# RetNet attention then SwiGLU, one core: five places for raw weights, other places of loads, stores and one product in the order of work

## The chip, the cores and the metric

The kernel runs on one core of a Trainium2 chip. The metric is the device time in microseconds (us) of one execution; times of several executions are given as a median with lowest and highest. A profile is one more execution with the hardware profiler on: it gives a span (first to last instruction) and every instruction's start and duration. The engines are TensorE (PE in the profile; its weight loads PEld), VectorE (DVE), ScalarE (ACT), GpSimd (POOL), and SyncE (SP), which here only issues transfers (its queue is SPq). Each engine works through its own list of instructions in order; a transfer is issued by a queue in order, too, and an instruction that waits holds everything behind it on that engine.

## The reference

Eight batches, eight heads, 576 positions, head size 64. All in 32-bit floats:

```python
scores = (q @ k.T) / 8                        # per batch and head
ret    = scores * gamma[h] ** (i - j)         # for i >= j, else 0
x      = ret @ v                              # -> (4608, 512), heads side by side
xn     = x / sqrt(mean(x*x) + 1e-6) * rms_g   # by row
g, val = xn @ w_gate, xn @ w_val              # 512 -> 1536
out    = (g * sigmoid(g) * val) @ w_out       # 1536 -> 512
```

## The kernel before

**Attention.** A job is one batch and a pair of heads: 32 jobs, numbered 0 to 31. A `slot(j)` (line 403) does `values(j-1)` (347, the product of weighted scores and v), `scores(j)`, `states(j)`, `weigh(j)` and then `carried(j-1)` (366), which adds the part that comes from earlier chunks of 64 positions, multiplies by the decay and writes the x of its unit of 512 tokens. `close(j)` (417) is values and carried of the last job of a batch. Carried must not begin before values has ended; this is told by a tiny copy named `tick` (361, 363): on GpSimd for jobs 0 to 7, on ScalarE afterwards. The loads of jobs 0 to 7 are issued at the start (`load_first`, `load_tails`); a later job is brought in by `fetch(j)` (421: 4 transfers for q, 4 for k in another layout, 2 for k, 2 for v, 1 for v's tail `vt`) and made ready by `prepare(j)` (251: two transposes on VectorE, four scalings of v on ScalarE by line 265). There is one place each for the raw q and k, so a fetch also waits for the prepare before it.

**Units.** Tokens are taken in nine units u of 512. Units 2 to 8 use Strassen-like products: `up(u, n)` (580) with seven products on precombined blocks of the gate and value weights, then `across(u)` (703) with seven pieces of the output weights. Those precombined blocks lie in device memory (`w_up_blocks`, `w_out_blocks`) and are loaded into a ring by `refill` (550), on SyncE, whenever a place is free. Units 0 and 1 are what the change is about.

**The plain stage.** The weights must first be rounded and combined, and units 0 and 1 meanwhile use plain products. The raw weights are cut into 36 half chunks (line 825): sets `up 0` to `up 5` of gate and value blocks and slices `out 0` to `out 2` of the output weights, four half chunks each. `load_half` (840) brings one raw half chunk into one of a few places, `spare`. Then, on VectorE: `exponent` (863), two activations on ScalarE (860), `mantissa` (877, three instructions), `join` (894, line 907). `rounding` (955) hands this out in steps; the order in it is: exponent of the next half chunk, mantissa of this one, join of this one. So three steps are one half chunk, and after join i the load for a later half chunk is issued by SyncE. When the fourth half chunk of a set or slice has been joined, GpSimd forms the sums (line 918; four instructions for a set, eight for a slice, through `finish_set` and `finish_slice`), and some joins later SyncE issues the stores to device memory (`store_blocks`, 937). All slices share one place in `vi`, and so the join of the next slice waits until the stores of the one before have landed.

The order of the work is written out by hand in `start()` (994); no planner is at work. First come slots 0 to 7 with some steps of rounding between (`weights(n)`). Then the twelve blocks of `up_plain(u, k)` (639) for units 0 and 1, four groups each, 48 in all; `now` numbers them. A group is four products of 128x128 by 512 columns; the profile shows a matmul as two records, so a group is eight records. For odd k VectorE multiplies the group's result (656), for even k ScalarE applies Silu (658). After each group come `weights(3)` and two activations; `weights_to(READY[k])` makes sure that the set for the block is joined. In the code:

```python
weights(3 if now > 3 else 1)
act(2)
if i == 1:
    weights_to(READY[k])
```

Some groups are followed by a prepare, a fetch or a slot for the jobs 8 to 11. After block (0, 5), that is after group 39, the rest of rounding and the last stores are put on the queues and then the first refill; the fetch of job 11 stands behind these on SyncE, after group 41, and job 11 is prepared after group 44 and has its slot after group 45. After group 47 comes the close of job 11, and `across(0)`.

**Later units.** For u = 2 to 6, `up(u, n)` with n = 0 to 3 is followed by a slot each, and n = 4 by the close of the last job of that batch (line 1144).

Of the kernel before, what the change touches and what calls it, by code (L numbers as in the profile page):

```python
# [10 lines left out]
F32 = mybir.dt.float32  # L11
# [30 lines left out]
def kernel(  # L42
# [44 lines left out]
    def bank(name):  # L87
        return banks.tile([P, 512], F32, tag="b", name=name)
# [7 lines left out]
    def cell(name, value):  # L96
# [34 lines left out]
    AT_SETS, N_SETS = NF * U, 3  # L131
    AT_SUMS = AT_SETS + N_SETS * 4 * BLOCK
    AT_RAW = AT_SUMS + 4 * BLOCK
    WORDS, SLOT = 2 * 4 * P, 3 * 4 * P
    assert AT_RAW + 2 * SLOT <= RING
    spare = [
        ring[:, AT_RAW : AT_RAW + SLOT], ring[:, AT_RAW + SLOT : AT_RAW + 2 * SLOT],
        t1.rearrange("p f t -> p (f t)"), sums_x.rearrange("p i c t -> p (i c t)"),
    ]

    A11, A12, S1, A22, S2, S3, S4 = range(7)
    A21 = 7
# [274 lines left out]
    def close(j):  # L417
        values(j)
        carried(j)

    def fetch(j):
        if j < len(jobs):
            load_qk(j)
            load_kv(j)
# [107 lines left out]

    UP, OUT = 7 * 2 * 2 * P, 7 * NK * P
    w_up_d = dram.tile([2 * NG, P, UP], F32, name="w_up_blocks")
    w_out_d = dram.tile([7, P, 7, NK, P], F32, name="w_out_blocks")
    ORDER = (A11, S1, S3, S2, A12, S4, A22)
    pieces = [("out", u, n) for u in range(2) for n in range(7)]
    for u in range(2, NU):
# [11 lines left out]
    def refill(most=len(pieces)):  # L550

        nonlocal n_sent
        while n_sent < min(most, len(pieces)):
            a, z = places[n_sent]
            if any(a < y and x < z for x, y in places[n_used:n_sent]):
                return
            kind, u, n = pieces[n_sent]
            src = w_up_d[n] if kind == "up" else w_out_d[ORDER[n]].rearrange("p n c d -> p (n c d)")
            nc.sync.dma_start(out=ring[:, a:z], in_=src)
            n_sent += 1  # L560

    def piece(kind, u, n):
        assert pieces[n_used] == (kind, u, n) and n_used < n_sent
        a, z = places[n_used]
        if kind == "up":
            return ring[:, a:z].rearrange("p (b c f) -> p b c f", b=7, c=2)
        return ring[:, a:z].rearrange("p (n c d) -> p n c d", n=7, c=NK)

    def used():
        nonlocal n_used  # L570
# [253 lines left out]
    slices = vi[:, : 49 * P].rearrange("p (o n d) -> p o n d", o=7, n=7)  # L824
    halves = []
    for kind, at in (
        ("up", 0), ("up", 1), ("up", 2), ("out", 0), ("up", 3), ("out", 1), ("up", 4), ("up", 5),
        ("out", 2),
    ):
        halves += [(kind, at, a, c) for a in range(2) for c in range(2)]  # L830

    def words_of(i):
        return spare[i % 4][:, :WORDS].bitcast(U32)

    exps = {}

# [25 lines left out]

    def exponent(i):

        exps[i] = bank(f"exp_{i}") if in_psum else spare[i % 4][:, WORDS:]
        w, e = words_of(i), exp_of(i).bitcast(U32)
        nc.vector.tensor_scalar(
            out=e, in0=w[:, 1::2], scalar1=20, scalar2=0x7FF,
            op0=ALU.logical_shift_right, op1=ALU.bitwise_and,
        )  # L870
        f = exp_of(i)
        acts.extend((i, x) for x in (
            dict(out=f, in_=e, bias=most, scale=-1.0),
            dict(out=e, in_=f, bias=top, scale=-(2.0**23)),
        ))
# [56 lines left out]
    def finish_slice(k):  # L932
        combine_blocks([slices[:, i, :4] for i in range(7)], S1)
        combine_blocks([slices[:, :, i] for i in range(7)], S1)
        stores.append((n_joined + 5, [(w_out_d[o][:, :, k], slices[:, o]) for o in ORDER]))

    def store_blocks(n):

# [16 lines left out]
    def rounding():  # L955

        nonlocal n_joined
        exponent(0)
        yield
        for i in range(len(halves)):  # L960
            if i + 1 < len(halves):
                exponent(i + 1)
            yield
            mantissa(i)
            yield
            while not free_for(*halves[i][:2]):
                assert not due
                yield
            join(i)
            n_joined += 1  # L970
            store_blocks(n_joined)
            load_half(i + 4, nc.sync)
            yield

    steps = rounding()
# [1 line left out]
    def weights(n):  # L977

        for _ in range(n):
            next(steps, None)  # L980
# [6 lines left out]
            next(steps)  # L987
        due = False

    READY = (4, 8, 12, 20, 28, 32)  # L990

    def start():
# [12 lines left out]
        warm_up(6)  # L1007
        for i in (1, 0, 2):
            table(i, nc.scalar)
        load_half(0, nc.scalar)  # L1010
        for j in range(FIRST):
            load_first(j)
            if j == 0:
                load_tails(0, range(2))
                table(3, nc.sync)
            elif j == 1:
                load_tails(0, range(2, H))
                load_half(1, nc.sync)
            elif j == 5:
                load_half(3, nc.sync)  # L1020
            elif j == 3:
                load_half(2, nc.sync)
                nc.sync.dma_start(out=rms_g, in_=moe_rms_g.rearrange("(c p) -> p c", p=P))
            elif j == 4:
                load_tails(1, range(H))
                table(4, nc.sync)
        turn(0, 1)
        scale_v(0)
        squares = []
        weights(1)  # L1030
        for j in range(FIRST):
            slot(j, rest=(j > 0))
            if j + 1 < FIRST:
                turn(j + 1)
            if squares:
                gather(*squares.pop())
            for i in ((1,), (2,), (3,), (4, 5), (6,), (7,), (), ())[j]:
                scale_v(i)
            if j:
                squares.append((*divmod(j - 1, NHP), square(*divmod(j - 1, NHP))))  # L1040
            act(1)
            if j == 5:
                norm_1(0)
            elif j == 6:
                norm_2(0)
            weights((1, 1, 2, 2, 1, 1, 1, 1)[j])
            if j == 4:
                gather(*squares.pop())
            elif j == 5:
                diagonals(0)  # L1050
            act(1)
# [4 lines left out]
        for u, k in (  # L1056
            (0, 0), (1, 0), (0, 1), (1, 1), (0, 2), (1, 2), (0, 3), (1, 3), (0, 4), (0, 5), (1, 4),
            (1, 5),
        ):
            weights_to(READY[k] - 2)  # L1060
            for i, _ in enumerate(up_plain(u, k)):
                if now == 0:
                    close(FIRST - 1)
                    gather(1, NHP - 1, square(1, NHP - 1))
                elif now == 1:
                    norm_1(1)
                elif now == 2:
                    diagonals(1)
                elif now == 3:
                    norm_2(1)  # L1070
                elif now in (10, 16):
                    prepare(FIRST + (now - 10) // 6)
                elif now in (12, 18):
                    fetch(FIRST + 1 + (now - 12) // 6)
                elif now == 34:
                    slot(FIRST, rest=False)
                elif now in (40, 42, 45):
                    slot(FIRST + {40: 1, 42: 2, 45: 3}[now])
                elif now in (41, 44, 46):
                    n = {41: 2, 44: 3, 46: 4}[now]  # L1080
                    prepare(FIRST + n)
                    fetch(FIRST + n + 1)
                elif now == 47:
                    close(FIRST + NHP - 1)
                weights(3 if now > 3 else 1)
                act(2)
                if i == 1:
                    weights_to(READY[k])
                now += 1
            sets_used[k] += 1  # L1090
            if (u, k) == (0, 5):
                weights_to(len(halves))
                store_blocks(len(halves) + 9)
                refill(1)
            elif (u, k) == (1, 4):
                refill(2)
                for f in range(0, NH, 2):
                    differences(0, f)
                inner_sums(0, 0)
                inner_sums(0, 1)  # L1100
# [22 lines left out]
    with tc.manual_schedule():  # L1123
        start()
        for u in range(2, NU):
            j0 = NHP * (u + 1)
            more = u + 1 < B
            for n in range(2 * NG):
                for i, _ in enumerate(up(u, n)):
                    if n == 1 and i == 4:  # L1130
                        store(u - 1)
                    if more and i == 2 and 0 < n <= NHP:
                        if j0 + n < len(jobs):
                            prepare(j0 + n)
                            fetch(j0 + n + 1)
                    if u + 1 < NU and n == 2 * NG - 1:
                        if i < NHP:
                            gather(u + 1, i, square(u + 1, i))
                        elif i == NHP:
                            root_1(u + 1)  # L1140
                if more and n < NHP:
                    slot(j0 + n, rest=(n > 0))
                elif more and n == NHP:
                    close(j0 + NHP - 1)
            for i, _ in enumerate(across(u)):
                if u + 1 == NU:
                    continue
# [33 lines left out]
```

## Time and profile before

| | us |
|---|---|
| median of 8 runs (lowest, highest) | 1160.27 (1158.23, 1163.93) |
| the profiled execution's own time | 1161.05 |
| its span | 1159.3 |
| TensorE busy | 1108.3 (96%) |
| VectorE busy | 822.0 (71%) |
| GpSimd busy | 400.5 (35%) |
| ScalarE busy | 247.8 (21%) |
| mean granted TensorE clock | 0.982 |

How to read it. The slices show the span in 40 equal parts of 29 us; each digit is the busy share in tenths, 9 for 90% or more; PEclk is the clock that TensorE was granted, in tenths of full speed. In a list of instructions in order of time, a row has the start, the duration, engine, line, operation, what it writes and reads, the shape, how many instructions are merged in it, and in brackets how long the engine was idle before the first of them and what ended that. A merged row runs from its first start to its last end. TensorE's instructions overlap, so a row ends 0.28 us after the next product could have begun. VectorE's instructions of 128x512 are shown with 0.69 us but start 0.60 apart. In a row of SPq the duration is that of issuing, not of the transfer.

### The profile page before, as it was taken

How to read it: one execution, taken by the hardware profiler on the slowest of the kernel's cores; microseconds unless marked ns; L12 is line 12 of the kernel's file. 1: busy time of each engine (PE TensorE's matmuls, PEld its weight loads, DVE VectorE, ACT ScalarE, POOL GpSimd, SP SyncE). 2: the span in 40 equal slices, each digit the busy share in tenths (PEclk: the TensorE clock that was granted, in tenths of full speed). 3: DMA queues.
4: the chain of work that ended last, by engine and by line, in shares of the span. 5: the costliest groups of instructions: out<-in, count | busy, mean ns of one | idle time of the engine just before them, and what ended most of it. 6: DMA issues, size and time to landing. Idle time of an engine off the chain costs nothing. (4 is left out here: it accounts for less than half of the span.)

```text
span 1159.3 us, 24137 instructions
## 1 busy us (share of the span) xinstructions
PE 1108.3 (96%) x10086; PEld 919.4 (79%) x10086; DVE 822.0 (71%) x1426; ACT 247.8 (21%) x501; POOL 400.5 (35%) x328
## 2 busy tenths in 40 slices
PE   7899777998999999999999999999999999999997
PEld 6744333457998889888988899889988998898897
DVE  4899857667696769576947795779576954593465
ACT  5534422211002120123012301221212111201110
POOL 0023524543752018301730164006500660174035
PEclk9999888998999999999999999999999999999999
DMA  8648898388887887578668875897576556475461
GB/s 211 158 111 259 223 292 265 117 217 252 313 305 228 233 246 252 159 202 217 265 210 222 247 247 183 196 256 265 191 178 238 194 194 223 143 272 177 159 238 38
DMA packets 255421, 249.22 MB, mean 215 GB/s; under 512 B 193104, under 2 KB 232656, under 8 KB 241104
## 3 DMA queue, kind: packets, MB, share of 16 engines
q1 hardware_dynamic: 253456, 246.59, 68.5%
q8 instruction: 79, 1.29, 0.5%
q10 hardware_dynamic: 1856, 1.09, 0.3%
q14 instruction: 30, 0.25, 0.1%
HBM read 217.55 MB, written 30.08 MB: 214 GB/s over the span
## 5 line engine op out<-in xcount | busy, mean ns | idle before, releaser
L701 POOL TENSOR_TENSOR vi<-h 128x384 f32<-128x384 f32 x64 | 77.6, 1229 | 502.5 <-DVE h L608 456.8
L650 PE MATMUL up<-x,ring 128*128 128x512 f32 x384 | 178.0, 622 | 19.9 <-DVE ring L656 9.2
L650 PEld LDWEIGHTS up<-x,ring 128*128 128x128 f32 x384 | 74.9, 199 | 117.6 <-issue 85.0
L589 PE MATMUL x<-x,ring 128*128 128x256 f32 x672 | 161.5, 383 | 0.8 <-issue 0.8
L589 PE MATMUL z<-x,ring 128*128 128x256 f32 x672 | 158.8, 379 | 0.0
L589 PE MATMUL w<-sums,ring 128*128 128x256 f32 x672 | 158.7, 379 | 0.0
L589 PEld LDWEIGHTS z<-x,ring 128*128 128x128 f32 x672 | 127.7, 190 | 19.9 <-issue 2.9
L589 PEld LDWEIGHTS w<-sums,ring 128*128 128x128 f32 x672 | 127.7, 190 | 17.4
L589 PEld LDWEIGHTS x<-x,ring 128*128 128x128 f32 x672 | 125.1, 190 | 18.4 <-issue 1.0
L589 PE MATMUL y<-sums,ring 128*128 128x256 f32 x336 | 79.4, 379 | 0.0
L802 POOL TENSOR_TENSOR vi<-vi 128x512 f32<-128x512 f32 (+1 forms) x56 | 67.2, 1213 | 22.1 <-DVE vi L748 19.6
L596 DVE TENSOR_TENSOR h<-u,w 128x512 f32<-128x512 f32 x42 | 28.9, 688 | 61.1 <-PE w L589 61.1
L589 PEld LDWEIGHTS y<-sums,ring 128*128 128x128 f32 x336 | 63.8, 190 | 8.7
L615 ACT COPY m<-x 128x512 f32<-128x512 f32 x42 | 24.6, 586 | 189.1 <-PE x L589 189.1
L596 DVE TENSOR_TENSOR u<-m,y 128x512 f32<-128x512 f32 x42 | 28.8, 686 | 50.2 <-PE y L589 50.2
L333 DVE SCALAR_TENSOR_TENSOR sum<-sum,gc,s 128x64 f32<-128x64 f32 x192 | 53.9, 281 | 6.8
L610 ACT ACTIVATE h<-h 128x512 f32<-128x512 f32 x63 | 39.7, 630 | 79.8 <-DVE h L596 79.8
L918 POOL TENSOR_TENSOR vi<-vi 128x512 f32<-128x512 f32 (+1 forms) x24 | 40.3, 1681 | 45.8 <-DVE vi L907 20.5
L744 ACT COPY vi<-xo 128x512 f32<-128x512 f32 x18 | 10.6, 587 | 211.3 <-PE xo L730 178.6
L596 DVE TENSOR_TENSOR u<-u,z 128x512 f32<-128x512 f32 x42 | 28.9, 687 | 26.7 <-PE z L589 25.7
L701 POOL TENSOR_TENSOR vi<-h,vi 128x384 f32<-128x384 f32 x32 | 46.3, 1447 | 2.5
L918 POOL TENSOR_TENSOR ring<-ring 128x512 f32<-128x512 f32 x24 | 30.5, 1278 | 46.8 <-DVE sums L890 31.2
(252 smaller groups left out, 2001.1 us busy)
## 6 DMA issues: line engine op xcount, KB each, us to landing
ring<-w_out_blocks SPq DMA_DIRECT2D x63, 1344.0 KB, 6.7
ring<-w_up_blocks SPq DMA_DIRECT2D x42, 1792.0 KB, 7.9
w_out_blocks<-vi SPq DMA_DIRECT2D x21, 448.0 KB, 6.0
out_dram<-vi SPq DMA_DIRECT2D x64, 128.0 KB, 3.1
qraw<-in_q_dram SPq DMA_DIRECT2D x96, 72.0 KB, 5.2
kraw<-in_k_dram SPq DMA_DIRECT2D x96, 72.0 KB, 3.1
k<-in_k_dram SPq DMA_DIRECT2D x48, 128.0 KB, 3.0
v<-in_v_dram SPq DMA_DIRECT2D x48, 128.0 KB, 3.0
```

The costliest lines, as they stand in the source:

```text
L333: nc.vector.scalar_tensor_tensor(out=t[:, c], in0=t[:, c - 1], scalar=gc[:, hp : hp + 1], in1=part, op0=ALU.mult, op1=ALU.add,)
L589: nc.tensor.matmul(ps[:, i * HU : i * HU + HU], lhsT=w[:, PLACE[blk], c, i * P : i * P + P], rhs=t_of[u][blk][:, c], start=(start and i == ...
L596: nc.vector.tensor_tensor(out=o, in0=a, in1=pairs_of(ps), op=ALU.add)
L610: nc.scalar.activation(out=o, in_=c, func=AF.Silu)
L615: nc.scalar.copy(out=s1, in_=pairs_of(x_))
L650: nc.tensor.matmul(ps, lhsT=w[:, PLACE[blk], c % 2, i * P : i * P + P], rhs=x_of[u][:, c], start=(c == 0), stop=(c == NHP - 1),)
L701: eng.tensor_tensor(out=o, in0=a, in1=b, op=op)
L744: nc.scalar.copy(out=o, in_=ps)
L802: eng.tensor_tensor(out=t[:, :, o], in0=t[:, :, x], in1=t[:, :, y], op=ALU.add)
L918: nc.gpsimd.tensor_tensor(out=t[o], in0=t[x], in1=t[y], op=op)
```

## The change

- The raw weights have five places instead of four, each without room for its exponents; before the exponents go to PSUM, they use two other places in turn. A load is then issued five half chunks ahead.
- The order of half chunks: slice `out 0` comes before set `up 2` instead of behind it, so half chunks 8 to 11 instead of 12 to 15. `READY` is adjusted for `up 2`.
- `w_out_blocks` is laid out with the slice ahead of the partition: a store of a slice writes 128 rows of 3584 B instead of 896 rows of 512 B, and a refill reads three rows per partition instead of one.
- At the start, half chunk 0 is loaded by SyncE behind the loads of job 1 instead of by ScalarE ahead of all; the other first loads move too, and the tails of jobs 4 to 7 come one job sooner.
- The steps of rounding are dealt out otherwise: none by slots 0 and 1, then 1, 2, 2, 2, 1, 2; in the plain stage two and three in turn instead of three.
- `prepare(8)` and `fetch(9)` move from groups 10 and 12 to group 28; `prepare(9)` and `fetch(10)` from 16 and 18 to 36.
- In units 2 to 6, the values of a batch's last job are issued ahead of the last product of `up(u, 4)` and only the carried part follows it, in place of the close.

```diff
-    WORDS, SLOT = 2 * 4 * P, 3 * 4 * P
...
+    WORDS = 2 * 4 * P
+    assert AT_RAW + 3 * WORDS <= RING
+    flat_t = [t1.rearrange("p f t -> p (f t)"), sums_x.rearrange("p i c t -> p (i c t)")]
+    spare = [ring[:, AT_RAW + i * WORDS : AT_RAW + i * WORDS + WORDS] for i in range(3)]
+    spare += [t[:, :WORDS] for t in flat_t]
+    N_RAW = len(spare)
...
-    w_out_d = dram.tile([7, P, 7, NK, P], F32, name="w_out_blocks")
+    w_out_d = dram.tile([7, NK, P, 7 * P], F32, name="w_out_blocks")
...
-            src = w_up_d[n] if kind == "up" else w_out_d[ORDER[n]].rearrange("p n c d -> p (n c d)")
-            nc.sync.dma_start(out=ring[:, a:z], in_=src)
+            o = ring[:, a:z]
+            if kind == "up":
+                src = w_up_d[n]
+            else:
+                o = o.rearrange("p (c x) -> p c x", c=NK)
+                src = w_out_d[ORDER[n]].rearrange("c p x -> p c x")
+            nc.sync.dma_start(out=o, in_=src)
...
-        ("up", 0), ("up", 1), ("up", 2), ("out", 0), ("up", 3), ("out", 1), ("up", 4), ("up", 5),
+        ("up", 0), ("up", 1), ("out", 0), ("up", 2), ("up", 3), ("out", 1), ("up", 4), ("up", 5),
...
-        stores.append((n_joined + 5, [(w_out_d[o][:, :, k], slices[:, o]) for o in ORDER]))
+        stores.append((n_joined + 5, [
+            (w_out_d[o][k], slices[:, o].rearrange("p n d -> p (n d)")) for o in ORDER
+        ]))
...
-            load_half(i + 4, nc.sync)
+            load_half(i + N_RAW, nc.sync)
...
-    READY = (4, 8, 12, 20, 28, 32)
+    READY = (4, 8, 16, 20, 28, 32)
...
-        load_half(0, nc.scalar)
...
-                load_half(1, nc.sync)
-            elif j == 5:
-                load_half(3, nc.sync)
-            elif j == 3:
-                load_half(2, nc.sync)
+                load_half(0, nc.sync)
+            elif j in (2, 4, 5, 7):
+                load_half({2: 1, 4: 2, 5: 3, 7: 4}[j], nc.sync)
+            if j == 3:
                 nc.sync.dma_start(out=rms_g, in_=moe_rms_g.rearrange("(c p) -> p c", p=P))
-            elif j == 4:
                 load_tails(1, range(H))
...
-        weights(1)
...
-            weights((1, 1, 2, 2, 1, 1, 1, 1)[j])
+            weights((0, 0, 1, 2, 2, 2, 1, 2)[j])
...
-                elif now in (10, 16):
-                    prepare(FIRST + (now - 10) // 6)
-                elif now in (12, 18):
-                    fetch(FIRST + 1 + (now - 12) // 6)
+                elif now == 28:
+                    prepare(FIRST)
+                    fetch(FIRST + 1)
+                elif now == 36:
+                    prepare(FIRST + 1)
+                    fetch(FIRST + 2)
...
-                weights(3 if now > 3 else 1)
+                weights((3 - now % 2) if now > 3 else 1)
...
+                    if more and n == NHP and i == 5:
+                        values(j0 + NHP - 1)
...
-                    close(j0 + NHP - 1)
+                    carried(j0 + NHP - 1)
```

More of the change, by code (lines that the diff above doesn't have):

```diff
@@ L133 @@
     AT_RAW = AT_SUMS + 4 * BLOCK
-    WORDS, SLOT = 2 * 4 * P, 3 * 4 * P
[L135 to L139, printed above, removed]
+    WORDS = 2 * 4 * P
[4 more added lines that the diff above has]
+    N_RAW = len(spare)
     A11, A12, S1, A22, S2, S3, S4 = range(7)
@@ L566, in piece @@
             return ring[:, a:z].rearrange("p (b c f) -> p b c f", b=7, c=2)
-        return ring[:, a:z].rearrange("p (n c d) -> p n c d", n=7, c=NK)
+        return ring[:, a:z].rearrange("p (c n d) -> p n c d", n=7, c=NK)
     def used():
@@ L832, in words_of @@
     def words_of(i):
-        return spare[i % 4][:, :WORDS].bitcast(U32)
+        return spare[i % N_RAW].bitcast(U32)
     exps = {}
@@ L863, in exponent @@
     def exponent(i):
-        exps[i] = bank(f"exp_{i}") if in_psum else spare[i % 4][:, WORDS:]
+        exps[i] = bank(f"exp_{i}") if in_psum else flat_t[i % 2][:, WORDS:]
         w, e = words_of(i), exp_of(i).bitcast(U32)
```

## The prediction

> **What bounds the kernel now.** I read the page's slices first, then TensorE's instructions in order of time, then the same for VectorE, SyncE's queue and ScalarE. TensorE is busy nearly everywhere; the hole lies between 120 and 210 us, and the granted clock dips after each gap.
>
> ```profile
> PE   7899777998999999999999999999999999999997
> PEclk9999888998999999999999999999999999999999
> ```
>
> Those are the twelve blocks of plain up products (48 groups, numbered by `now`; eight records a group). In order of time:
>
> ```profile
> 77.78 45.63 PE L650 MATMUL up<-x,ring 128*128 128x512 f32 x104 [0.84 <-DVE x L515]
> 126.03 3.70 PE L650 MATMUL up<-x,ring 128*128 128x512 f32 x8 [2.61 <-DVE ring L656]
> 132.99 20.29 PE L650 MATMUL up<-x,ring 128*128 128x512 f32 x40 [3.26 <-DVE ring L907]
> 155.61 5.40 PE L650 MATMUL up<-x,ring 128*128 128x512 f32 x8 [2.34 <-DVE vi L907]
> 165.09 29.43 PE L650 MATMUL up<-x,ring 128*128 128x512 f32 x64 [4.08 <-DVE vi L907]
> 201.11 13.49 PE L650 MATMUL up<-x,ring 128*128 128x512 f32 x24 [6.59 <-DVE ring L656]
> ```
>
> Five waits of 18.9 us for VectorE. The second row is at full clock: (3.70 - 0.28)/8 = 0.4275 us a record, 3.43 a group. Against that, 40 records take 2.9 us too long, the next 8 1.7, 64 1.8, 24 3.0: 9.4 us of slow clock. VectorE in turn waited for transfers:
>
> ```profile
> 122.77 0.69 DVE L867 TENSOR_SCALAR exp<-ring 128x512 uint32<-128x512 uint32 x1 [2.45 <-DMA ring<-in_moe_w_val_dram]
> ...
> 150.54 0.42 DVE L907 SCALAR_TENSOR_TENSOR vi<-ring,exp 128x256 f32<-128x256 f32 x1 [5.31 <-DMA w_out_blocks<-vi]
> ...
> 161.64 0.69 DVE L867 TENSOR_SCALAR exp<-sums 128x512 uint32<-128x512 uint32 x1 [6.08 <-DMA sums<-in_moe_w_out_dram]
> ...
> 197.85 0.70 DVE L867 TENSOR_SCALAR exp<-sums 128x512 uint32<-128x512 uint32 x1 [6.65 <-DMA sums<-in_moe_w_val_dram]
> ```
>
> SyncE's queue says why. The raw loads stand behind long issues: a fetch (13 transfers, 109.40 to 117.1), and seven stores of an output slice, 9 us each time. The last of them ends the stage:
>
> ```profile
> 145.21 9.30 SPq L941 DMA_DIRECT2D w_out_blocks<-vi  x7
> 154.61 1.33 SPq L853 DMA_DIRECT2D sums<-in_moe_w_out_dram  x1
> ...
> 234.83 9.85 SPq L941 DMA_DIRECT2D w_out_blocks<-vi  x7
> 244.78 0.62 SPq L559 DMA_DIRECT2D ring<-w_out_blocks  x1
> 245.76 4.06 SPq L159 DMA_DIRECT2D qraw<-in_q_dram  x4
> ```
>
> Behind these stores stands the fetch of job 11, and it is only just in time: ScalarE scales its v the moment it lands, and TensorE waits 0.77 us for that.
>
> ```profile
> 258.80 0.51 ACT L265 ACTIVATE v<-v,gv 128x256 f32<-128x256 f32 x1 [6.34 <-DMA v<-in_v_dram]
> 260.30 0.35 ACT L265 ACTIVATE vt<-vt,gv 64x64 f32<-64x64 f32 x1 [0.99 <-DMA vt<-in_v_dram]
> ```
>
> **Places, order, rate (plain stage).** A half chunk costs VectorE 0.60 (exponent) + 1.95 (mantissa) + 0.65 (join) = 3.2 us, from starts in the rows at 168 to 172. Three steps a group is 3.2, or 3.8 with the product of L656, against TensorE's 3.43; the new 2.5 steps are 2.7 or 3.3, so VectorE follows TensorE. With four places, a load is issued two joins before its exponent, 2 x 3.43 = 6.9 us; with five, three joins of 1.2 groups each, 12.3 us. Landing takes 4 to 7. `out 0` becomes half chunks 8 to 11, its stores go out at 16 joined, and `out 1` writes the slices from 20 on: four joins (16 us) where there were none, so the 5.3 us wait goes. The sets of up blocks stay in time: set 2 is half chunks 12 to 15, the last joined some 7.4 us after group 15, when its second product in group 18 needs it at 8.5. I remove all five waits: -18.9, and with them the slow clock.
>
> Here the Trainium skill (TensorE: Matmul & The Clock Gate, Part 1) is less generous: half clock comes after an idle window of about 3.4 us, so by it only the 4.08 and 6.59 waits cost clock, at 1.7 us each (3.4 us of half rate). The rows show half clock also after 3.26 and 2.34, and up to 3.0 us each. I take the rows, -9.4; by the rule it is -3.4 and the end comes 6 us later.
>
> **Fetches moved to groups 28 and 36.** Each is two transposes (1.4 us VectorE), four scalings and 13 issues. At 28, SyncE is held for 1.4 + 7.8 us, so half chunk 29's load goes out about 9.2 us after group 28 and lands at 14.7 (5.5 landing, as at 117.18 to 122.7); VectorE wants it at 13.4. That is 1.3 us, part of it swallowed by the idle ahead of slot 8: +1 on TensorE (0 to 3). At 36 no raw load is left behind it.
>
> **Attention stage.** Half chunk 0's load leaves ScalarE's queue and stands in SyncE's behind job 1; early slots start 1 to 2 us sooner. But ScalarE's scaling of job 6 waited for v until 43.65 and VectorE behind it 3.96 us until 45.58, and the bytes ahead of that load are the same; the gain dies there. After it VectorE has man 1, join 1 and exponent 3 more than before (1.75 + 0.60 + 0.35, with 0.2 of reordering): +2.9, and VectorE was idle only 2.4 us from there to the x of unit 1. I take +3 (0 to +4.5) and 1.5 (0 to 3) for the clock after that gap.
>
> End of group 39: 233.1 before (215.74 + 20.87 - 0.28 - 3.43, rounded); after, 233.1 - 18.9 - 9.4 + 3 + 1.5 + 1 = 210.3.
>
> **The tail moves the other way.** Before, the last half chunk was joined at 222.0, before group 36 ended. Now VectorE's work of groups 36 to 39 is 5.2 + 3.3 + 3.9 + 6.6 = 19.0 us, begun 0.5 after group 36's end, i.e. at 210.3 - 10.3 + 0.5: the last join ends at 219.5. GpSimd's seven sums follow (12.60 at 222.21): 232.2. So the last stores start only 2.6 us sooner than at 234.83, though TensorE is 23 ahead. Job 11's fetch waits on SyncE behind them.
>
> Long rows help here. Seven issues of 128 rows cost what the stores of w_up cost, 0.43 each: 3.0 for 9.85. The data, 7 x 448 KB = 3.2 MB, went at 285 GB/s (windows 236 to 247), 11.3 us; the nearest rows with longer runs are raw loads, 403 GB/s in the window 120 to 123: 8.0. With the first store's landing to be awaited, job 11's vt lands 21.6 us after the stores start instead of 25.5: 253.8. The skill (DMA: Bandwidth & Descriptors, Specifications) puts full rate at 512 B and up, which is what the short rows already were; by it the data takes 11.3 us still and everything here is 3 later. I take the rows.
>
> TensorE reaches slot 11 near 238 and waits 13 to 15 us. Group 46 then starts 1.9 after vt, at 255.7 instead of 262.19: -6.5. From there to `across(0)`: two groups 7.1, about 3 of half clock, values and carried 1.8 = 11.9, against 11.7 before, which held a 2.79 us wait for v of job 12 (its new fetch, issued at about 251, lands under these groups). The half clock that before hit the first products of `across(0)`, 3 us (12 records in 2.93 us for 1.50, and on to 278), falls into that stretch: -3. Net for the stage: -6.5 + 0.2 - 3 = -9.3. Job 13's fetch and the later pieces keep their distance behind it.
>
> **Values ahead, later units.** Five closes (u = 2 to 6) each end in this wait:
>
> ```profile
> 416.67 0.69 PE L374 MATMUL av<-qT,sum 64*64 64x64 f32 x32 [0.79 <-ACT tick L363]
> ```
>
> With the last product (1.73 us) between, ScalarE's tick comes after the Silu at 414.18, about 1 us before it is needed: 5 x 0.8 = -4.0. The 63 output pieces now read three rows of 3584 B per partition: nothing, as SyncE's waits are for TensorE to free the ring; uncovered, rival 3 below.
>
> **Sum.** -9.3 - 4.0 = -13.3 on the profiled execution's 1161.05 (span 1159.3): 1147.7; the runs' median is 0.8 below that execution, so 1147.
>
> **Rivals.** 1. The tail is hidden: if job 11's fetch were in time, `across(0)` would follow group 39 by 36.1 us (8 groups, three slots of 2.25, close 1.9) instead of 40.8: -22.8 - 4.7 - 3 - 4 = -34.5, 1126. For it: TensorE's own pace. Against: that fetch had no slack before. Half of it gives about 1137.
> 2. The change does part of what it says: raw loads still come late behind the slices' stores, a third of the 28.3 us of waits and clock remains, 9.4 us, and passes whole to the start of the last stores: 1156. For it: two stores and two fetches still share the queue with the loads. Against: 12.3 us of lead.
> 3. Slower: the moved fetches jam the last raw loads. The two such jams before cost VectorE up to 6.65; twice that with 3 us clock each is 19 us on the tail's start, 1166. It decides once the last stores start 13 us later than I have them, at 245.5. Against: only loads 29 to 32 stand behind a fetch. (Output pieces in three rows could do the same only below 280 GB/s, 0.22 us on each of 63; the raw loads' 403 at 2 KB rows speaks against.)
>
> **How the numbers follow.** Mine 0.62, own range 1139 to 1155 (clock by the rule +6, short-row rate +3, attention 0 to +4.5); rival 1 0.13; rival 2 0.12, a third of it within 0.2% (2.3 us, about what this kernel's runs can tell); rival 3 0.13. Leaving out rival 3 and the far end of rival 1: 1134 to 1160. Faster 0.83, within 0.04, slower 0.13.
>
> **What would show it.** Right: no TensorE wait over 2 us between 80 and 205; store issues of about 3 us; the last stores starting near 232; one TensorE wait of 13 to 15 us for slot 11, ended by job 11's k or v; no tick waits after 300. Wrong: VectorE still waiting for raw loads, a first product of unit 1 later than 84, or slot 11 without a wait.

## The result, and the profile after

The changed kernel takes 1152.81 us (median of 11 runs, 1149.67 to 1154.97) against 1160.23 us before (32 runs, 1156.98 to 1163.93). The ratio is 0.9932, 95% interval 0.992 to 0.9943 (the quotient of the two medians, 0.9936, lies in it): faster by 0.7%. Predicted were 1147.0 us, with 1134 to 1160 as the range. So the sign and the range held, but of the 13.3 us that the sum promised only 7.4 came.

The profiled execution of the changed kernel took 1155.67 us, 2.9 above its median; its span is 1153.9 us, 5.4 shorter than before. TensorE's busy time and its granted clock in the 40 slices of the page:

```profile
PE   7889999959999999999999999999999999999997
...
PEclk8989999989999999999999999999999999999999
```

The ragged stretch between 120 and 210 us is gone. One low digit, 5, stands in its place (the slice from 230.8 to 259.6 us), and in the first slices the digits are 788 where they were 789. TensorE's instructions from the end of the attention stage on, in order of time:

```profile
75.61 1.02 PE L447 MATMUL ms<-mean_w,sq 128*128 128x1 f32 x8 [1.92 <-DVE sq L440]
...
80.14 7.51 PE L655 MATMUL up<-x,ring 128*128 128x512 f32 x12 [0.93 <-DVE ring L912]
89.44 106.67 PE L655 MATMUL up<-x,ring 128*128 128x512 f32 x248 [0.93 <-DVE x L515]
197.46 20.87 PE L655 MATMUL up<-x,ring 128*128 128x512 f32 x48
...
256.53 1.35 PE L284 MATMUL s<-qT,kT 64*64 64x64 f32 x40 [11.99 <-DVE kT L256]
...
260.93 9.29 PE L655 MATMUL up<-x,ring 128*128 128x512 f32 x16
...
283.53 1.58 PE L735 MATMUL wo<-ring,h 128*128 128x128 f32 x12 [1.96 <-DMA ring<-w_out_blocks]
323.03 0.94 PE L735 MATMUL wo<-ring,vi 128*128 128x128 f32 x6 [1.53 <-POOL vi L706]
```

Read three things from it. The row at 89.44 is one unbroken run of 248 records, 31 groups, at (106.67 - 0.28)/248 = 0.429 us a record, full clock: all five waits of VectorE's joins are gone. But it begins at 89.44, where group 4 began at 77.78 before; the rows at 75.61 and 80.14 show waits for VectorE that were not there. And one wait of 12 us stands at slot 11. Group 39 ends at 197.46 + 20.87 - 0.28 - 3.43 = 214.6. Before, the same sum is 215.74 + 20.87 - 0.28 - 3.43 = 232.9; the prediction's 233.1 is 0.2 too late.

The tail, from GpSimd's last sums over SyncE's queue to ScalarE's scalings for job 11:

```profile
223.97 12.62 POOL L923 TENSOR_TENSOR vi<-vi 128x512 f32<-128x512 f32 x7 [5.39 <-issue]
```

```profile
236.62 6.02 SPq L948 DMA_DIRECT2D w_out_blocks<-vi  x7
242.74 1.05 SPq L564 DMA_DIRECT2D ring<-w_out_blocks  x1
243.84 4.51 SPq L159 DMA_DIRECT2D qraw<-in_q_dram  x4
```

```profile
256.93 0.51 ACT L265 ACTIVATE v<-v,gv 128x256 f32<-128x256 f32 x1 [19.36 <-DMA v<-in_v_dram]
258.23 0.35 ACT L265 ACTIVATE vt<-vt,gv 64x64 f32<-64x64 f32 x1 [0.79 <-DMA vt<-in_v_dram]
```

The last stores start at 236.62, later than the 234.83 of before, although TensorE finished group 39 18.3 us sooner. Of these 18.3 us 2.0 are left at the first product of `across(0)` (271.92 against 273.90). Most of the loss is the 12 us at slot 11, which waits for the fetch behind those stores; another 2.4 us are two waits of slot 9, at 220 to 223 us, for VectorE, which is still rounding then.

The row at 323.03 stood at 325.07 before, so the start, the plain stage and the tail together gave 2.0 us in this execution; the remaining 3.4 of the span's 5.4 come later. There the list of TensorE's waits had, from 330 us on, as its largest entry before

```profile
PE av L374 <- ACT tick L363: 4.0, 5, 0.8
```

and the changed kernel's list has no entry for the tick there.

### The profile page after: what moved, and what is told of

Same layout as the page of the kernel before. It is cut to its first block, busy times and chain, and to the rows that moved or that the text cites. A ratio compares the mean times of both kernels' runs of the same rounds, so it can differ in the third digit from the quotient of the medians.

```text
span 1153.9 us, 24145 instructions
## 1 busy us (share of the span) xinstructions
PE 1104.9 (96%) x10086; PEld 918.5 (80%) x10086; DVE 823.2 (71%) x1426; ACT 247.4 (21%) x501; POOL 399.1 (35%) x328
## 5 line engine op out<-in xcount | busy, mean ns | idle before, releaser
L655 PE MATMUL up<-x,ring 128*128 128x512 f32 x384 | 172.2, 608 | 2.0 <-DVE ring L912 0.9
L594 PEld LDWEIGHTS z<-x,ring 128*128 128x128 f32 x672 | 127.7, 190 | 19.9 <-issue 2.9
L594 PEld LDWEIGHTS x<-x,ring 128*128 128x128 f32 x672 | 125.1, 190 | 18.3 <-issue 0.9
L317 DVE SCALAR_TENSOR_TENSOR ret<-s,causal 128x320 f32<-128x320 f32 x64 | 28.8, 485 | 29.5 <-PE s L284 22.4
L601 DVE TENSOR_TENSOR u<-u,z 128x512 f32<-128x512 f32 x42 | 28.9, 687 | 26.7 <-PE z L594 25.7
## 6 DMA issues: line engine op xcount, KB each, us to landing
out_dram<-vi SPq DMA_DIRECT2D x64, 128.0 KB, 3.0
k<-in_k_dram SPq DMA_DIRECT2D x48, 128.0 KB, 3.0
v<-in_v_dram SPq DMA_DIRECT2D x48, 128.0 KB, 2.9
```

Source lines behind the costliest of these rows:

```text
L317: nc.vector.scalar_tensor_tensor(out=ret[:, e], in0=s[e][:, : n * L].rearrange("p (c k) -> p c k", k=L), scalar=float(_gamma(H)[2 * hp + e ...
L594: nc.tensor.matmul(ps[:, i * HU : i * HU + HU], lhsT=w[:, PLACE[blk], c, i * P : i * P + P], rhs=t_of[u][blk][:, c], start=(start and i == ...
L601: nc.vector.tensor_tensor(out=o, in0=a, in1=pairs_of(ps), op=ALU.add)
L655: nc.tensor.matmul(ps, lhsT=w[:, PLACE[blk], c % 2, i * P : i * P + P], rhs=x_of[u][:, c], start=(c == 0), stop=(c == NHP - 1),)
```

## The experiments

Each is compared with runs of the kernel before on the same chip; its ratio is to be set against the 0.9932 of the whole change, and 0.001 is 1.16 us. Two experiments whose ratios are less than about 0.002 apart can't be told apart by their intervals.

**1. The attention stage as before.** The changed kernel, with the loads and the steps of slots 0 to 7 put back (half chunk 4, which only the five places need, is loaded behind job 7).

```diff
+        load_half(0, nc.scalar)
...
-                load_half(0, nc.sync)
-            elif j in (2, 4, 5, 7):
-                load_half({2: 1, 4: 2, 5: 3, 7: 4}[j], nc.sync)
-            if j == 3:
+                load_half(1, nc.sync)
+            elif j in (5, 7):
+                load_half({5: 3, 7: 4}[j], nc.sync)
+            elif j == 3:
+                load_half(2, nc.sync)
                 nc.sync.dma_start(out=rms_g, in_=moe_rms_g.rearrange("(c p) -> p c", p=P))
+            elif j == 4:
...
+        weights(1)
...
-            weights((0, 0, 1, 2, 2, 2, 1, 2)[j])
+            weights((1, 1, 2, 2, 1, 1, 1, 1)[j])
```

> The changed kernel, with the first loads and the steps of slots 0 to 7 as before the change (half chunk 0 on ScalarE's queue, steps 1 then 1,1,2,2,1,1,1,1; half chunk 4 loaded behind job 7). Theory A: the changed attention stage delivers group 4 at 89.4 instead of 77.8 us, and these 11.7 us pass whole to the last stores, which are paced by group 39: group 4 near 79, the last stores near 226, time 1152.8 - 9 to 11 = 1142 to 1144. Rival B: the 12 us wait ahead of slot 11 is set by something else and swallows a sooner start: the wait grows and the time stays at 1151 to 1154.

Measured: 1141.20 us (1139.03 to 1146.06), ratio 0.9835 (0.982 to 0.985), 11.2 us better than the whole change (0.0097 x 1159). TensorE in order of time:

```profile
77.91 12.28 PE L655 MATMUL up<-x,ring 128*128 128x512 f32 x28 [0.84 <-DVE x L515]
...
246.26 1.35 PE L284 MATMUL s<-qT,kT 64*64 64x64 f32 x40 [13.23 <-DVE kT L256]
...
313.54 0.94 PE L735 MATMUL wo<-ring,vi 128*128 128x128 f32 x6 [1.53 <-POOL vi L706]
```

Group 4 starts 11.5 us sooner, slot 11 10.3, the row of line 735 9.5. This profiled execution took 1146.06 us, 4.9 above the median, as the one of the whole change lay 2.9 above its own. A delay at the start passes nearly whole through the plain stage and the tail.

**2. Only the loads as before**, the steps left as the change has them.

> The changed kernel with only the first loads as before; the steps of slots 0 to 7 stay as changed (none for slots 0 and 1). Tells the two parts of the attention stage apart. If the loads are what made it later (TensorE's unexplained waits of 3.4, 1.5 and 2.1 us and its half clock at 16 to 26 us come from two raw loads close together ahead of job 3): group 4 near 82, time 1145 to 1147. If the steps are (more VectorE work after slot 4, and mantissa close behind its exponent): group 4 stays at 87 to 90, time 1151 to 1153.

Measured: 1151.70 us (1150.23 to 1152.88), ratio 0.9938 (0.9924 to 0.9953), no better than the whole change. Group 4 starts at 83.99, between the two expectations; with the new loads it starts at 84.75 and 84.89 in the fourth and the fifth experiment, so this one start does not decide. By the times it is the steps that cost: with them either way of loading is slow. The old steps with the new loads were not run. VectorE's longest wait here:

```profile
39.70 0.69 DVE L887 SCALAR_TENSOR_TENSOR t<-ring,t 128x512 uint32<-128x512 uint32 x1 [5.99 <-ACT t L865]
```

This is mantissa 0, waiting for its own two activations. With two steps behind slots 3 and 4 it follows close on exponent 0, and ScalarE, in whose queue the activations stand, has scalings of v ahead of them (one waits until 37.15 for its v). The changed kernel has the same wait, 4.37 us at 43.05. How much work is left over then shows in the windows of 0 to 45 and 45 to 78 us (columns: length, then busy time and number of instructions on PE, PEld, DVE, ACT and POOL, clock, DMA share, GB/s), first before, then after, then this kernel:

```profile
0.00:45.00 45.00, 35.31 (x902) 29.79 (x904) 25.73 (x82) 24.48 (x64) 1.26 (x11) 0.94 0.88 210
45.00:78.00 33.00, 30.96 (x467) 19.73 (x464) 28.99 (x76) 13.10 (x28) 8.12 (x9) 0.98 0.44 105
```

```profile
0.00:45.00 45.00, 32.37 (x758) 27.40 (x760) 18.20 (x62) 19.68 (x52) 1.28 (x10) 0.87 0.83 203
45.00:78.00 33.00, 29.01 (x591) 20.71 (x592) 30.45 (x88) 15.27 (x34) 2.80 (x6) 0.97 0.35 90
```

```profile
0.00:45.00 45.00, 33.89 (x856) 28.67 (x860) 21.13 (x72) 22.39 (x60) 1.13 (x11) 0.96 0.90 215
45.00:78.00 33.00, 27.82 (x507) 19.21 (x500) 30.70 (x82) 12.80 (x26) 5.43 (x7) 0.96 0.38 90
```

Up to 45 us VectorE does 25.7 us of work before, 18.2 after and 21.1 here, attention and rounding together; from there on it is 88 to 93% busy in all three. It has little room to catch up: the 7.5 or 4.6 us not done in the early idle time stand ahead of the x of unit 1 later.

**3. Only the values ahead of the product**, put into the kernel before.

```diff
+                    if more and n == NHP and i == 5:
+                        values(j0 + NHP - 1)
...
-                    close(j0 + NHP - 1)
+                    carried(j0 + NHP - 1)
```

> The kernel before, with only the values of the last job ahead of the last product. Theory: the five waits of 0.8 us on ScalarE's tick go, nothing else moves: 1160.2 - 4.0 = 1156.2, ratio 0.9966. Rival: the wait is swallowed or taken up by a later one (POOL's sums, the refill): 1159 to 1161.

Measured: 1155.70 us (1152.66 to 1158.13), ratio 0.997 (0.9959 to 0.998): 3.5 us, with no tick wait after 330 us.

**4. Three steps a group again** in the plain stage.

```diff
-                weights((3 - now % 2) if now > 3 else 1)
+                weights(3 if now > 3 else 1)
```

> The changed kernel with three steps of rounding after every group, as before, in place of three and two. Theory: the last half chunk is joined around group 36 to 37 instead of 9 us behind group 39, the last stores start 9 to 11 us sooner (near 227) and so does all behind them; the wait ahead of slot 11 shrinks to a few us: 1143 to 1146. Rival: at three steps VectorE needs 3.8 us a group in the blocks that it also multiplies, against 3.43, and TensorE waits in the plain stage again, 5 us or more: 1150 to 1156.

Measured: 1145.66 us (1143.69 to 1147.79), ratio 0.9887 (0.9871 to 0.9903): better than the whole change by 5.2 us. TensorE and then SyncE:

```profile
180.98 11.13 PE L655 MATMUL up<-x,ring 128*128 128x512 f32 x24 [1.32 <-DVE ring L661]
196.20 6.14 PE L655 MATMUL up<-x,ring 128*128 128x512 f32 x8 [4.10 <-DVE vi L912]
204.31 20.87 PE L655 MATMUL up<-x,ring 128*128 128x512 f32 x48 [0.76 <-ACT h L663]
```

```profile
223.61 6.38 SPq L948 DMA_DIRECT2D w_out_blocks<-vi  x7
```

The waits in the plain stage are back, 7.0 us in four, because VectorE is ahead and again stands before transfers (3.66 and 2.23 us for the last raw loads). Yet the stores start 223.61 - 84.75 = 138.9 us after group 4, where they started 236.62 - 89.44 = 147.2 after it, and slot 11 no longer waits. What ends the stage is VectorE's last join, not TensorE; slowing VectorE to remove TensorE's waits was a loss. Both expectations came true in part: TensorE waits as the rival had it, and the time is the theory's.

**5. Job 11's fetch ahead of the last stores** and the first refill, in the changed kernel.

```diff
                     fetch(FIRST + n + 1)
+                    if now == 41:
+                        store_blocks(len(halves) + 9)
+                        refill(1)
...
-                store_blocks(len(halves) + 9)
-                refill(1)
```

> The changed kernel, with the last stores of an output slice and the first refill put on SyncE's queue behind job 11's fetch instead of ahead of it. Theory: the 12 us wait ahead of slot 11 is head-of-line blocking on SyncE: job 11's fetch then needs only job 10's transposes (230 us), lands near 241, and slot 11 goes without a wait over 2 us; what is left is the wait for job 12's v ahead of the last carried part, behind the stores and refills: across(0) near 261 instead of 272, time 1152.8 - 10 = 1143. Rival: the stores and the first output pieces themselves are late: the wait moves to across(0), gain under 3 us, 1150 to 1153.

Measured: 1144.64 us (1143.90 to 1147.67), ratio 0.9883 (0.9866 to 0.9899). The wait at slot 11 is gone, and there is a new one, on TensorE and then on ScalarE:

```profile
259.97 1.14 PE L374 MATMUL av<-qT,sum 64*64 64x64 f32 x32 [10.37 <-ACT tick L363]
```

```profile
258.11 0.51 ACT L265 ACTIVATE v<-v,gv 128x256 f32<-128x256 f32 x1 [17.56 <-DMA v<-in_v_dram]
```

The tick of job 11's close is queued on ScalarE behind the scaling of job 12's v, whose fetch is now the one behind the stores. The queueing moved on by one job; 5.7 us were left of it.

**6. Short rows**: the old layout of `w_out_blocks` (rows of 512 B) in the changed kernel.

```diff
-    w_out_d = dram.tile([7, NK, P, 7 * P], F32, name="w_out_blocks")
+    w_out_d = dram.tile([7, P, 7, NK, P], F32, name="w_out_blocks")
...
-            (w_out_d[o][k], slices[:, o].rearrange("p n d -> p (n d)")) for o in ORDER
+            (w_out_d[o][:, :, k], slices[:, o]) for o in ORDER
```

> The changed kernel with the old layout of the output blocks: stores of 896 rows of 512 B, refills of one row per partition. Theory: the last seven stores take 11.3 us of transfer for 8.0 and issue in 9 to 10 us for 6.0, so job 11's vt lands 3.5 to 4 us later behind them and all that follows: 1156 to 1157. If rows of 512 B are at full rate already: 1152 to 1153.5. If the refills in three rows cost something in the later units, this kernel is faster than the changed one: under 1152.

Measured: 1155.20 us (1153.44 to 1158.64), ratio 0.9971 (0.9959 to 0.9983): the long rows are worth 4.5 us, give or take 2, a little less than the theory had. While the last stores go out, the windows of the changed kernel and of this one read

```profile
238.00:244.00 6.00, 6.00 (x30) 2.54 (x32) 4.23 (x7) 0.00 (x0) 1.33 (x2) 1.00 1.02 402
```

```profile
237.00:244.00 7.00, 6.57 (x50) 2.94 (x48) 4.26 (x7) 0.00 (x0) 0.04 (x1) 1.00 1.03 284
```

with the transfer engines full in both (1.02, 1.03) and 402 against 284 GB/s moved. From the stores' start to slot 11 it is 19.9 us with long rows and 22.75 with short ones. The Trainium skill (DMA: Bandwidth & Descriptors, Specifications) would have both at full rate; the measurement decides against that here.

**7. The first and the fifth together**: the attention stage as before, and the fetch ahead of the stores.

> Both together on the changed kernel: attention stage as before, and the last stores behind job 11's fetch. Theory: the two losses follow each other (the start sets group 39, the queue sets what comes after), so the gains add: 1141.2 - 10 = 1131. Rival: they overlap (with an earlier group 39 the fetch, the stores and job 12's loads meet in the transfers): 1137 to 1141.

Measured: 1136.08 us (1135.14 to 1136.77), ratio 0.9806 (0.979 to 0.9822). The two gains, 11.2 and 5.7 us, add to 14.6 of 16.9, which the intervals can't tell from the whole; the time lies between the 1131 of the theory and the 1137 to 1141 of the rival. The wait for the tick is there again, 10.66 us at 251.46.

**8. Four places.** The changed kernel with four of its five places in use.

```diff
-    N_RAW = len(spare)
+    N_RAW = 4
...
-            elif j in (2, 4, 5, 7):
-                load_half({2: 1, 4: 2, 5: 3, 7: 4}[j], nc.sync)
+            elif j in (2, 4, 5):
+                load_half({2: 1, 4: 2, 5: 3}[j], nc.sync)
```

> The changed kernel with four places for raw weights instead of five (half chunk 4 loaded after join 0). A load is then issued two joins of 1.2 groups ahead, 8.2 us, for landings of 4 to 7 and stores of 5 to 7 us in the queue before some. Theory: VectorE waits 3 to 5 us at two to four loads that stand behind a slice's stores or a fetch; half of it is swallowed by TensorE's lead of two groups: group 39 1 to 5 us later, 1154 to 1159. Rival: the order and the rate alone removed the waits and the fifth place is not needed: 1152 to 1154.

Measured: 1155.34 us (1151.20 to 1158.90), ratio 0.9975 (0.996 to 0.9989): the fifth place is worth 5.0 us, give or take 2. VectorE waits for raw loads again, 5.07 us at the longest, and the last stores start at 238.42, so slot 11's wait (10.25 us) ends later, at 258.72 instead of 256.53.

**9. Job 12 taken off the close's way.** To the seventh kernel: the preparation of job 12 and the fetch of job 13 behind the first fetches of output pieces.

```diff
-                elif now in (41, 44, 46):
-                    n = {41: 2, 44: 3, 46: 4}[now]
+                elif now in (41, 44):
+                    n = {41: 2, 44: 3}[now]
...
             differences(1, f)
+        prepare(FIRST + NHP)
+        fetch(FIRST + NHP + 1)
```

> Edit: the kernel with the old start and job 11's fetch ahead of the last stores (1136.1), and in it the preparation of job 12 (which no slot of the start needs) and the fetch of job 13 put behind the last fetch of output pieces, after the slots of the start. Theory A (with the fetch moved, TensorE's 10.7 us before the carried products of job 11 are job 12's scaling of v, which stands ahead of the small ScalarE operation that they wait for): the wait falls to under 2 us, the first inner products start near 244 in place of 252.5, time 1126 to 1130. Rival (the inner products then wait for their output pieces, whose fetches start no earlier than the last stores are over, at about 239, and for the last joins' own chain): waits of 4 us or more on pieces at the start of across(0), or the piece for the second inner product late, and 1132 to 1136. Slower than 1136 if job 12's late data stall the first slot of the next part.

Measured: 1138.50 us (1136.12 to 1139.28), ratio 0.981 (0.9797 to 0.9824): not faster than the seventh. The tick wait is gone (0.35 us) and the first inner products start at 244.79, as theory A had it, but nothing is left of the gain:

```profile
270.23 2.90 PE L735 MATMUL yo<-ring,h 128*128 128x128 f32 x12 [9.10 <-DMA ring<-w_out_blocks]
```

Neither theory's time was right. The rival's mechanism was, at another piece than it named: this is the fourth output piece (the next expectation calls it the third), and on SyncE it stands behind job 13's fetch. A time above 1136 had been expected only with a stall of the next part's first slot, and the profile has no such wait.

**10. Job 13's fetch behind seven pieces**, in `across(1)`; the cut is against the ninth kernel.

```diff
-        prepare(FIRST + NHP)
-        fetch(FIRST + NHP + 1)
...
+            elif i == 3:
+                prepare(FIRST + NHP)
+                fetch(FIRST + NHP + 1)
             elif i == 4:
                 root_2(2)
```

> Edit: the kernel with the old start and job 11's fetch ahead of the last stores (1136.1), with job 12's preparation and job 13's fetch put into the inner products of sequence 1, behind the fetches of the first seven output pieces. In the run with them put only behind the slots (1138.5) the wait for the tick was gone and the first inner products started 8 us sooner, but TensorE then waited 9.1 us at 270 us for the third output piece, which was queued behind job 13's fetch (issued over 9 us from 254.6). Theory A (that queueing is the wait, on the path): no wait over 3 us for a piece, the last third starts about 9 us sooner than in the run before, time 1128 to 1131. Rival (the pieces of sequence 0 themselves bound this stage, each held until its place in the ring is free): pieces still waited for, 6 us or more in sum, and 1134 to 1139.

Measured: 1134.02 us (1133.30 to 1137.32), ratio 0.979 (0.9772 to 0.9808), the lowest median of all: 2.1% under the kernel before, but not to be told from the seventh (0.9806) by the intervals. TensorE still waits for pieces:

```profile
257.17 2.90 PE L735 MATMUL wo<-ring,h 128*128 128x128 f32 x12 [5.06 <-DMA ring<-w_out_blocks]
...
310.64 1.58 PE L735 MATMUL zo<-ring 128*128 128x128 f32 x12 [1.40 <-DMA ring<-w_out_blocks]
```

That is 6.5 us in sum, and the time lies where the rival had it, at 1134 to 1139: theory A falls. Once both job 11's and job 12's data are out of the way, TensorE waits for output pieces in this stretch. The first of the two rows is the third piece: SyncE issued it at 250.75, right behind the last transfer of job 12's fetch (250.05, 0.61 long), so the queue held it until then at least. Whether its place in the ring was free sooner was not shown.

## Why the prediction was right in sign and short in size

The predicted steps, against the changed kernel's profile:

| step | predicted | measured |
|---|---|---|
| attention stage, start of group 4 | +4.5 | +11.7 |
| group 4's start to end of group 39 (155.1 before) | 128.0 | 125.2 |
| end of group 39 to last join's end | 9.2 | 9.2 |
| GpSimd's last sums | 12.6 | 12.6 |
| issue of the last seven stores | 3.0 | 6.0 |
| stores' start to job 11's vt | 21.6 | 21.6 |
| wait at slot 11 | 13 to 15 | 12.0 |
| job 11's vt to group 46 | 1.9 | 2.7 |
| group 46 to `across(0)` | 11.9 | 11.0 |
| `across(0)` to the row at 323.03, against before | -3 | -0.1 |
| start, plain stage and tail together | -9.3 | -2.0 |
| values ahead | -4.0 | -3.4 |

The failed step is the attention term, "+3 (0 to +4.5) and 1.5 (0 to 3) for the clock". Over the profiled executions, group 4 started at 84.0 to 89.4 in the six kernels with the new steps (mean 86.5) and at 76.3 to 77.9 in the six with the old ones, before among them (mean 77.1): 9.4 us. By the times, undoing the stage gave 11.2. Taken without that term, the predicted sum was -13.3 - 4.5 = -17.8; the first experiment, the change without its new start, gave 0.0165 x 1158.84 = -19.1. So by the medians the rest of the sum was right to about a microsecond, and this one term is as large as the whole miss. That the rest came out so well is partly luck, as the table shows: the plain stage was 2.8 us shorter than predicted, and the stretch from `across(0)` to the row at 323.03 came out 2.9 us longer. There the half clock saved 2.3 us of the 3, and the third output piece, which the prediction had at nothing, came 1.96 us late (the row at 283.53). One of the prediction's own signs of failure, unit 1's first product later than 84, showed it.

What the step left out: it counted the instructions that VectorE had more behind 45 us (one mantissa, one join, one exponent, 2.9 us). It took VectorE's wait there, 3.96 us for ScalarE, as given and as the end of any earlier loss. After the change another wait stands there, for the mantissa's own activations (4.1 to 8.3 us in the six executions), and up to 45 us VectorE is 3.8 to 7.5 us of work behind and not 2.9. It then has 10% of free time at most, and TensorE waits for its squares (1.92 us), its join (0.93) and its x. That the mantissa's wait is what puts VectorE behind is read from the profiles; no run changes it alone.

The profiles also show where the delay arises. The last carried product of the attention stage, that of job 7, starts at 63.41 before and at 68.91 after the change:

```profile
63.41 1.15 PE L374 MATMUL av<-qT,sum 64*64 64x64 f32 x32 [0.28 <-POOL tick L361]
```

```profile
68.91 1.15 PE L374 MATMUL av<-qT,sum 64*64 64x64 f32 x32 [0.27 <-POOL tick L361]
```

So 5.5 of the 11.7 us are lost by then; in the other five executions with the new steps it is 1.0 to 3.7. From there to group 4 it is 14.4 us before and 18.5 to 20.9 in all six, 4.2 to 6.5 more. This second part, VectorE's work left over, is there every time. The first part varies: it is largest, 5.5 and 3.7 us, in the two executions whose granted clock in the window of 16 to 30 us was lowest, 0.63 and 0.69 (the changed kernel and the sixth experiment).

Of the rivals, none took the place of the likeliest case. Rival 2 came close in time, 1156 for 1152.8, but not in mechanism: no wait for a join remained in the plain stage past group 4. Rival 3's jam did not come: behind the fetch at group 28 VectorE lost nothing, so the +1 for it was 0. Rival 1, 21 us below the prediction's own 1147, needed job 11's fetch in time. With that (the fifth experiment) 5.7 us came, since job 12 then stood where job 11 had stood; even with the old start and job 12 out of the way the kernel stopped at 1134, not at 1126.

Where row and rule were weighed, the rows held both times. The whole 9.4 us of slow clock went: the stage came out 2.8 us shorter than predicted, where the rule of the Trainium skill (TensorE: Matmul & The Clock Gate, Part 1) would have made it 6 longer. About 1 us of the 2.8 is the moved fetch that cost nothing, and 1.4 is a reading: products could have begun 0.28 us before the end of the row ahead, so each of the five waits cost 0.28 more than its bracket (77.78 + 45.63 - 0.28 = 123.13, and the next row starts at 126.03: 2.90, not 2.61). And the bytes of the stores moved faster in long rows, worth 4.5 us.

Where the prediction asked too little: it took the rate of 2.5 steps as one more part that removes waits. The fourth experiment shows that this part costs 5.2 us, since the last join sets the stores and these set slot 11. The prediction had the tail's arithmetic right, save that the seven stores took 6.0 us to issue and not 3.0, which moved nothing behind them; but it did not ask what three steps would give there.

## What to carry to other kernels

When waits of the busiest engine go away, follow what the next transfer hangs on: here a join on VectorE, a sum on GpSimd, stores and a fetch in one queue set the end of the stage, and 7 us of waits taken from TensorE were worth less than 8 us taken from that chain (the fourth experiment). Work that is put off from a stretch where an engine idles into one where it is full cost more than its length here: 2.9 us had been counted, and group 4 came 9.4 us later, in part, as the profiles read, because it had to wait for the other engine's queue at its new place. Count the backlog at the point where the engine becomes full, not the instructions behind it. And a queue that is cleared of one late item shows the next one: removing the 12 us wait gave 5.7 us, and removing the 10.7 us wait that followed gave nothing clear of noise, as job 12 and then the output pieces took its place.

## What had not been expected of the hardware

TensorE seems to wait for its own instructions at times. In the first 45 us it has waits for which the profile shows no releaser ("issue"), and they differ from one execution to the next. The page of every one of the twelve profiles counts transfers of a kind of their own (number, MB, share of the transfer engines):

```profile
q8 instruction: 79, 1.29, 0.5%
```

That is 79 transfers of 16 KB each, which come to 64 B for each of TensorE's 10086 products and 10086 weight loads. Over the twelve profiles there are 44 waits above 0.3 us without a releaser, 32 of them in the first 45 us, and every one of them ends 1.2 to 1.7 us after such a transfer has ended. The longest of the changed kernel is one:

```profile
20.76 0.59 PE L304 MATMUL s<-h 64*64 64x64 f32 x12 [3.42 <-issue]
```

The transfer ahead of it starts at 18.11 and takes 1.23 us. So these look like waits for the next block of TensorE's instructions; that is read from the times, and no run tests it. Most of the 79 transfers have no such wait behind them, and why a block comes late was not found.

With the same attention code these waits were at most 3.42 us in the changed kernel, 1.81 in the fourth experiment and 2.33 in the fifth, and the granted clock of the window 16 to 30 us was 0.63, 0.97 and 0.95. Group 4 began at 89.44, 84.75 and 84.89. With the old start the longest such wait was 1.13 to 1.84 us. The late group 4 of the changed kernel's profiled execution, 3 us over the mean of its like, goes with that execution being 2.9 us above the median; that the waits cause it is only argued.

Seven stores of 128 rows of 3584 B took 4.9 to 7.3 us to issue in the changed kernel, not 7 x 0.43, and of 896 rows of 512 B 9.2 to 9.9 in the kernel before and 8.5 to 11.1 in the sixth experiment: a seventh of the rows saves about a third of the issue. Full transfer engines moved 402 GB/s in the one form and 284 in the other.
